# Two smaller last chunks, and Q placed by DMA, in a fused attention and MLP kernel

## The chip, the cores and the metric

The kernel runs on one core of one Trainium2 chip. The metric is the device time of the whole launch in microseconds (us). Lower is better. The kernel before took 1586.94 us, the median of three runs (1586.9, 1586.94 and 1588.01).

## The reference

The input is x, 2048 rows of 512 numbers in bf16. The same two blocks are applied twice, with the same weights both times, so there are two layers of "attention, then MLP":

```python
x = x + attention(layernorm(x))   # 32 heads of 16 numbers each
x = x + mlp(layernorm(x))         # 512 -> 1792, relu, -> 512
x = x + attention(layernorm(x))
x = x + mlp(layernorm(x))
```

```python
q, k, v = split(x @ wqkv)                      # wqkv: 512 x 1536
scores = einsum("hqd,hkd->hqk", q, k) * 16 ** -0.5
o = einsum("hqk,hkd->hqd", softmax(scores), v)
attention = o @ wo                             # wo: 512 x 512
mlp = maximum(h @ w1, 0) @ w2                  # w1: 512 x 1792, w2: 1792 x 512
```

All heads attend to all 2048 keys, so 2 x 32 x 2048 x 2048 scores have to be put through an exponential. That is 268 million of them, or 4096 blocks of 128 keys by 512 queries.

## The kernel before

**Engines.** TensorE (PE) does the products, ScalarE (ACT) does most of the exponentials, VectorE (DVE) does the rest of them with integer arithmetic on the bits (about one block in six), GpSimd (POOL) does small layer norm arithmetic and broadcasting DMAs, and the sync engine (SP) issues nearly all other DMAs. Each engine works through its own list in the order in which it is written. An instruction whose input is late holds up everything behind it on its engine.

**Chunks.** Queries are handled in chunks of 512 rows (`QS`). In the second layer (l = 1) the last 1024 rows are cut into four chunks of 256, numbered (1, 2) to (1, 5); `LAST` is 5. A chunk is gone through in four *runs*, one for each T in 0 to 3: a run holds the 128 columns of Q of eight heads. Each run has two *segments*, e = 0 and e = 1: the heads stand in pairs inside 32 partitions, and a segment works on one head of each pair. The buffer `qbuf[n % 2]` therefore holds Q twice, once with the odd heads masked to zero and once with the even ones. `q_masked` (line 676) writes both halves from the PSUM bank `ps_f` in one DVE operation of twice the width.

**The attention loop.** Each turn (a *slot*) of the loop from line 1267 takes three units of 128 keys by 512 scores in one group of 32 partitions. PE writes their scores (line 1396) to one of two PSUM tiles of three banks. ACT then takes the exponential of all three banks (a tile of 1536 columns), or of two (1024 columns) while DVE takes the third (line 1090 and the four steps from line 1131 on, for two blocks at a time: a *pair*). PE multiplies the results by V (line 983) into the bank `ps_o`. Where a chunk has 256 rows, a unit is two blocks of keys by 256 queries.

**The planner.** The order of all this is written out by the Python program itself, which keeps a model clock for PE, DVE and ACT. Products that are not attention (K, V, Q, the output projection, both MLP products) are cut into pieces that are put between the scores of the slots. `q_group` (682) is urgent as soon as the run before it begins. `h_group` (722) makes the first MLP product with weight tiles that SP loads in turn into four buffers (`load_w1`, 710). At the end of a segment `finish_segment` (867) copies `ps_o` to a buffer u, sends the row of sums through SP to a small tile, takes reciprocals there, sends them back, broadcasts them (POOL DMA at 927, or a shuffle on DVE at 937), and multiplies (913).

**The start.** The lines from 182 on load x and the weights. `load_w` (179) loads the K and Q columns of wqkv in one DMA of 512 KB each. Then come layer norm of the first 512 rows, transposes on PE, and the first K, Q and V products. On SP the order is: x, K's weights, x, `wo`, the 1792 KB of `w2` (195), four tiles of `w1` (714), and then the DMA transposes (571) of the normalised tiles `xnbuf[0..3]` of rows 512 on, which the DVE writes at line 528.

**The end.** After the last segment the code from line 1437 on finishes the last chunk of 256 rows without the planner: normalisation of the last segment, output projection, layer norm, and both MLP products, interleaved by tile of the hidden layer (lines 1501 to 1522), with all of `w1` kept in SBUF by then (`w1_last`).

Of the kernel before, what the change touches and what calls it, by code (L numbers as in the profile page):

```python
# [25 lines left out]
def kernel(  # L26
# [11 lines left out]
    P = 128  # L38
# [43 lines left out]
    X_ISSUE, X_LAG = 1400.0, 7500.0  # L82
    RSTD_LAG = 4000.0
    AHEAD = (8.0, 8.0)
    LATE = 0.0
# [22 lines left out]
    qmask = masks[:, 2:4]  # L108
    wqkv = sb([P, NDC, 3 * D], BF16, "wqkv")
    wo = sb([P, NDC, D], BF16, "wo")  # L110
# [67 lines left out]

    def load_w(engine, a):
        engine.dma_start(out=wqkv[:, :, a : a + D], in_=wq_src[:, :, a : a + D])  # L180

# [6 lines left out]
    nc.scalar.activation(out=warm[:], in_=warm[:], func=ACTF.Exp)  # L188
    load_w(nc.sync, D)
    load_w(nc.scalar, 0)  # L190
    load_x(nc.sync, (4, 5, 6, 7))
    load_w(nc.scalar, 2 * D)
    load_x(nc.sync, range(8, NTT))
    nc.sync.dma_start(out=wo[:], in_=A_wo[:, :].rearrange("(c p) f -> p c f", p=P))
    nc.sync.dma_start(out=w2[:], in_=B_w2[:, :].rearrange("(c p) f -> p c f", p=P))

    make_identity(nc, ident[:])
    for kb in range(NKB):
        nc.gpsimd.memset(vaug[0][kb][:, :, DH : DH + 2], 1.0)
    for kb in range(NKB - TPC):  # L200
        nc.gpsimd.memset(vaug[1][kb][:, :, DH : DH + 2], 1.0)


    wide = [True]
# [256 lines left out]
    HALF = TPC // 2  # L461
    for n in range(4):
        chunks[1, 2 + n] = (2 * TPC + n * HALF, HALF)
    LAST = 5

# [46 lines left out]
    def ln_root(tag, rows):  # L512
# [11 lines left out]
        stt(out=y, in0=t1, scalar=1.5, in1=y, op0=ALU.add, op1=ALU.mult)  # L524

    def ln_apply(tag, tt, i):
        n = ln_n(tag)
        nc.vector.tensor_scalar(
            out=xnbuf[i][:], in0=x_t[tt][:],
            scalar1=mv[n][:, i, 0:1], scalar2=ya_[n][:, i : i + 1],  # L530
            op0=ALU.subtract, op1=ALU.mult,
        )

    def ln_transpose(tag, i, b=None, at_bank=None):
        pt = bank().bitcast(BF16) if b is None else b
        for c in range(NDC):
            ins = nc.tensor.transpose(
                pt[:, c * P : (c + 1) * P], xnbuf[i][:, c * P : (c + 1) * P], ident[:]
            )
            if wide[0]:  # L540
                uses(ins, in_bank[0] if b is None else at_bank)
        mark(("xT", tag, i), "pe")
        return pt[:, 0 : NDC * P].rearrange("p (c f) -> p c f", c=NDC)
# [4 lines left out]
    def ln_rows(tag, tt, n, i):  # L548
# [10 lines left out]
        if i == n - 1:  # L559
# [6 lines left out]
            def apply(k):  # L566
                ln_apply(tag, tt + k, k)
                if not by_dma(tag):
                    return
                _, l, j = tag  # L570
                nc.sync.dma_start_transpose(
                    out=xnT[j][:, :, k * P : (k + 1) * P], in_=xnbuf[k][:]
# [13 lines left out]
    def ln_groups(tag, dst, at_column, n, war):  # L586
        groups = []
        for i in range(0, n, 2):
            hold = {}

            def piece(k):
                if not k % 2:
                    hold["b"] = bank()
                half = hold["b"].bitcast(BF16)[:, k % 2 * D : (k % 2 + 1) * D]
                ln_transpose(tag, k, half)
                if not k % 2:
                    return
                pt = hold["b"].bitcast(BF16).rearrange("p (i c f) -> p c i f", i=2, c=NDC)

                def fin():  # L600
                    a = at_column + (k - 1) * P
                    nc.vector.tensor_copy(
                        out=dst[:, :, a : a + 2 * P].rearrange("p c (i f) -> p c i f", i=2), in_=pt
                    )
                    for of in (k - 1, k):
                        mark(("xnT", tag, of))

                put_evac(609, fin)

            groups.append(  # L610
                group(
                    [(1.3, lambda k=k, piece=piece: piece(k)) for k in (i, i + 1)],
                    [("xT", tag, k) for k in (i, i + 1)] + [("xnT", tag, k) for k in (i, i + 1)],
                    [("xn", tag, k) for k in (i, i + 1)] + war,
                )
# [6 lines left out]
    def k_mms(T, j):  # L622
        return [(wqkv[:, c, D + T * P : D + (T + 1) * P], xnT[j][:, c, :]) for c in range(NDC)]

# [10 lines left out]
    def v_mms(kb):  # L635
        j, i = divmod(kb, TPC)
        return [
            (xnT[j][:, c, i * P : (i + 1) * P], wqkv[:, c, 2 * D : 3 * D]) for c in range(NDC)
        ]
# [29 lines left out]
    def q_mms(l, j, T):  # L669
        xj, a, w = columns(l, j)  # L670
        return [
            (wqkv[:, c, T * P : (T + 1) * P], xnT[xj][:, c, a : a + w]) for c in range(NDC)
        ]
# [8 lines left out]
    def q_group(n, l, j, T):  # L682
        xj, _, w = columns(l, j)
        cost = 90 + 2.09 * w

        def fin(b):
            q_masked(n, b, w)
            mark(("q", n))

# [20 lines left out]
    def load_w1(n):  # L710

        if n < len(chunks) * NF - NF + NW1:
            ft = n % NF
# [6 lines left out]
    w1_to_load = deque()  # L720

    def h_group(l, j, ft, war):
        n = (l * NQS + j) * NF + ft
        xj, a, w = columns(l, j)

        number = QS // w
        fts = range(ft, ft + number)
# [14 lines left out]
        def after():  # L742
            for f in range(number):
                load_w1(n + f + NW1)
            if w1_to_load:
                home, of = w1_to_load.popleft()
                nc.sync.dma_start(
                    out=home,
# [4 lines left out]
            [  # L753
                (w1buf[(n + f) % NW1][:, c, :], xnT[xj][:, c, a : a + w])
                for f in range(number) for c in range(NDC)
            ],
            fin, made_here,
            each(w // P, "xnT", ("ln2", l, j)) + war + [("w1", n + f) for f in range(number)],
            after=after, wide_by=w, sums=number,
        )  # L760
# [20 lines left out]
    def before(l, j):  # L781
# [3 lines left out]
        if not j:  # L785
            return 0, NQS - 1
        rows = chunks[l, j][0] % TPC
        return max(
            (l, b) for b in range(j)
            if chunks[l, b][1] == TPC or chunks[l, b][0] % TPC == rows  # L790
        )
# [3 lines left out]
    def rest_of_chunk(l, j):  # L795

        if (l, j) == (1, LAST - 2):
            for ft in range(NF):
                home = (
                    w1buf[((l * NQS + LAST) * NF + ft) % NW1] if ft < NW1  # L800
                    else (kt01 + kt2)[(ft - NW1) // 2][:, ft % 2, :].rearrange(
# [12 lines left out]
        )  # L814
        gs = [h_group(l, j, ft, war_h) for ft in range(0, NF, QS // w)]
        gs += [z_group(l, j, i) for i in range((l, j) == (1, LAST - 1), n)]
# [47 lines left out]

    sums_wait = [0]

    def finish_segment(sg, last):
# [16 lines left out]
        if n >= NU:  # L884
            run_until(("m", n - NU))
        u, r, c = ubuf[n % NU], rbuf[n % NU], cbuf[n % NU]
        lane = DH if e == 0 else DH - 1
# [32 lines left out]
        ended[l, j] = ended.get((l, j), 0) + 1  # L920
        quick = ended[l, j] == NT or sg["load"] is not None and sg["busy"]

# [39 lines left out]
        elif sg is segs[-2]:  # L962
            task(3100, direct_all, ots + [("m", n)], war + [("u", n)])
        else:
# [203 lines left out]
    for e in range(2):  # L1168
# [3 lines left out]
            op=ALU.add, axis=mybir.AxisListType.XY,  # L1172
        )
        nc.vector.tensor_scalar(
            out=qmask[:, e : e + 1], in0=mask[e], scalar1=SCALE * LOG2E * UNIT, scalar2=None,
            op0=ALU.mult,
# [382 lines left out]
```

The softmax here doesn't subtract the row's maximum and nothing guards it: scores larger than these inputs give would overflow.

## Time and profile before

The times come from one execution under the hardware profiler. Its span, from the first to the last instruction, is 1586.6 us; that execution took 1588.44 us as a whole, so 1.84 us lie outside the span.

| part of the span | us | ACT busy, us |
|---|---|---|
| start to the first exponential | 0 to 14.4 | 3.15 |
| first run of attention | 14.4 to 28.7 | 13.68 |
| attention, chunks of 512 for the most part | 28.7 to 1100 | 1066.34 |
| attention, chunks of 256 for the most part | 1100 to 1557.6 | 456.64 |
| after the last exponential | 1557.6 to 1586.6 | 5.55 |

| engine | busy, us | share of the span |
|---|---|---|
| ACT | 1545.3 | 97% |
| DVE | 1506.7 | 95% |
| PE | 1430.4 | 90% |
| POOL | 101.3 | 6% |

A busy PE is not PE at its peak[...]. "Idle before" in a row of the profile is time in which the engine stood still just before these instructions, and the name behind the arrow is what it waited for. The granted TensorE clock was 0.995 of full speed.

### The profile page before, as it was taken

To read this page: it belongs to the slowest core of one execution; us is meant where nothing else is said; L and a number is where in the kernel's file an instruction comes from. 1 tells how busy PE (TensorE), PEld (TensorE's weight loads), DVE (VectorE), ACT (ScalarE), POOL (GpSimd) and SP (SyncE) were. 2 spreads that over 40 slices of the span, in tenths; PEclk is the share of its full clock that TensorE was granted. 3 is DMA by queue.
4 is the path that set the end of the run, shared out by engine and by line. 5 is a ranking of instruction groups with operands and counts; after the bars stand their busy time and mean duration, and the time that the engine had idled before them with its cause. 6 is when DMAs were issued, how large, how long until landed. Compare 5 with 4: busy or idle time off the path is not lost.

```text
span 1586.6 us, 45174 instructions
## 1 busy us (share of the span) xinstructions
PE 1430.4 (90%) x19752; PEld 536.9 (34%) x19752; DVE 1506.7 (95%) x2910; ACT 1545.3 (97%) x1383; POOL 101.3 (6%) x240
## 2 busy tenths in 40 slices
PE   8888889998899989999899998888999999999898
PEld 3222223222233322322223222223334444544454
DVE  7899999999999999999899998899999999999994
ACT  7999999999999999999999999999999999999994
POOL 2000001001010010100100001001001000010100
PEclk9999999999999999999999999999999999999998
DMA  6001101111012120120101000000210111313030
GB/s 193 15 2 26 18 9 22 39 25 25 6 19 45 23 29 7 25 48 13 26 2 28 21 2 1 2 4 9 54 25 16 40 33 27 74 26 80 13 62 15
DMA packets 128885, 45.57 MB, mean 29 GB/s; under 512 B 117840, under 2 KB 125776, under 8 KB 128688
## 3 DMA queue, kind: packets, MB, share of 16 engines
q1 hardware_dynamic: 114752, 29.36, 8.6%
q0 software_dynamic: 12592, 12.02, 4.3%
q8 instruction: 154, 2.52, 0.7%
q10 hardware_dynamic: 1344, 1.31, 0.2%
q14 instruction: 43, 0.35, 0.1%
HBM read 24.38 MB, written 2.10 MB: 17 GB/s over the span
## 4 chain that ended last, share of the span: by engine, by line
ACT 81%; PE 8%; DVE 7%; issue 2%; DMA 1%; ACTq 0%; DVEq 0%
ACT e L1405 81%; PE ps_s L1396 3%; PE ps_f L446 2%; DVE lin L1090 2%; PE ps_o L983 2%; DVE step L1131 1%; PE ps_s L1458 1%; DVE cube L1146 1%; DVE cube L1142 1%; DMA wqkv<-in_A_wqkv_dram 1%; DMA r<-u 0%; DVE ht L736 0%; DVE q L676 0%; DVE ot L913 0%; DVE stats L481 0%
## 5 line engine op out<-in xcount | busy, mean ns | idle before, releaser
L1405 ACT ACTIVATE e<-ps_s 128x1536 bf16<-128x1536 f32 (+1 forms) x1366 | 1536.7, 1362 | 8.5 <-PE ps_s L1396 8.1
L1396 PE MATMUL ps_s<-q,ktp 32*128 32x512 bf16 (+1 forms) x6136 | 608.1, 341 | 112.4 <-ACT e L1405 99.2
L983 PE MATMUL ps_o<-e,vaug 128*32 128x512 bf16 (+1 forms) x4236 | 500.8, 346 | 14.1 <-DVE u L897 8.3
L1090 DVE TENSOR_SCALAR lin<-ps_s 128x512 int16<-128x512 f32 x702 | 478.3, 685 | 24.5 <-PE ps_s L1396 18.1
L1396 PEld LDWEIGHTS <-ktp 32*128 32x128 bf16 x6136 | 200.3, 92 | 563.6 <-issue 418.9
L1131 DVE TENSOR_SCALAR step<-lin 128x1024 int16<-128x1024 int16 x702 | 275.3, 419 | 1.9 <-PE ps_o L983 0.9
L983 PEld LDWEIGHTS <-vaug 128*32 128x32 bf16 x6052 | 173.8, 95 | 300.9 <-issue 282.2
L1142 DVE TENSOR_TENSOR cube<-step 128x1024 f16<-128x1024 bf16 x351 | 238.4, 683 | 1.6 <-PE ps_o L983 0.2
L1146 DVE TENSOR_TENSOR cube<-cube,lin 128x1024 bf16<-128x1024 f16 x351 | 238.0, 679 | 0.0
L446 PE MATMUL ps_f<-w,ht 128*32 128x512 bf16 x1624 | 151.6, 381 | 1.8 <-DVE x L768 0.5
L446 PE MATMUL ps_f<-xnT,w 128*32 128x512 bf16 (+1 forms) x2016 | 146.3, 345 | 5.8 <-DVE ht L736 3.6
L983 PE MATMUL ps_o<-step,vaug 128*32 128x512 bf16 (+1 forms) x884 | 151.0, 340 | 0.0
L983 PE MATMUL ps_o<-cube,vthird 128*32 128x512 bf16 (+1 forms) x836 | 148.9, 339 | 0.0
L983 PE MATMUL ps_o<-lin,vaug 128*32 128x512 bf16 (+1 forms) x884 | 125.9, 339 | 4.6 <-DVE u L897 3.2
L927 POOL DMA_DIRECT2D r<-u x59 | 43.1, 731 | 1168.6 <-DVE lin L1090 341.7
L446 PE MATMUL ps_f<-xnT,wqkv 128*32 128x512 bf16 (+1 forms) x1312 | 109.4, 365 | 6.2 <-DVE ktp L626 1.1
L446 PE MATMUL ps_f<-wo,ot 128*32 128x512 bf16 x960 | 90.3, 381 | 1.2 <-DVE x L700 1.2
L736 DVE TENSOR_SCALAR ht<-ps_f 128x512 bf16<-128x512 f32 x105 | 72.0, 685 | 2.3 <-PE ps_f L446 1.5
L446 PEld LDWEIGHTS <-w 128*32 128x32 bf16 x2016 | 57.5, 96 | 33.9 <-issue 18.7
L676 DVE TENSOR_TENSOR q<-ps_f,masks 128x1024 bf16<-128x1024 f32 (+1 forms) x51 | 53.6, 1052 | 9.1 <-PE ps_f L446 8.1
L446 PEld LDWEIGHTS <-ht 128*32 128x32 bf16 x1624 | 46.9, 96 | 25.3 <-issue 11.9
L983 PEld LDWEIGHTS <-vthird 128*32 128x32 bf16 x836 | 43.6, 95 | 33.5 <-issue 28.7
(103 smaller groups left out, 609.4 us busy)
## 6 DMA issues: line engine op xcount, KB each, us to landing
w<-in_B_w_dram SPq DMA_DIRECT2D x130, 128.0 KB
r<-u POOLq DMA_DIRECT2D x32, 256.0 KB, 7.3
r<-u POOLq DMA_DIRECT2D x27, 128.0 KB, 4.9
out_dram<-x SPq DMA_DIRECT2D x16, 128.0 KB
x<-in_A_x_dram SPq DMA_DIRECT2D x14, 128.0 KB
w<-in_B_w_dram SPq DMA_DIRECT2D x1, 1792.0 KB
ktp<-in_B_w_dram SPq DMA_DIRECT2D x10, 128.0 KB
wqkv<-in_A_wqkv_dram ACTq DMA_DIRECT2D x2, 512.0 KB
```

What stands on the lines that cost most here:

```text
L446: nc.tensor.matmul(out[cols], lhsT[:, cols], rhs, start=i % k == 0, stop=i % k == k - 1, tile_position=(0, 32 * g), skip_group_check=True,)
L676: return nc.vector.tensor_mul(out=qbuf[n % 2][:, :, 0:w], in0=b.rearrange("p (e q) -> p e q", e=1).to_broadcast((P, 2, w)), in1=qmask.rear ...
L736: nc.vector.tensor_scalar(out=out, in0=sums, scalar1=0.0, scalar2=None, op0=ALU.max)
L927: nc.gpsimd.dma_start(out=r[:, 0:width], in_=bass.AP(tensor=sums.tensor, offset=sums.offset, ap=[list(sums.ap[0]), [0, 32], [1, width]],),)
L983: nc.tensor.matmul(ps_o[32 * g : 32 * g + 32, 0 : sg["w"]], values[:, 4 * sg["T"] + g, 2 * e : 2 * e + 32], rhs, start=g not in sg["begun" ...
L1090: first = nc.vector.tensor_scalar(out=lin[which][:, half * QS : (half + 1) * QS], in0=src, scalar1=EXP_BIAS, scalar2=0.0, op0=ALU.add, op1 ...
L1131: nc.vector.tensor_scalar(out=stair, in0=line, scalar1=keep, scalar2=put, op0=ALU.bitwise_and, op1=ALU.bitwise_or,)
L1142: (609, lambda: nc.vector.tensor_mul(out=power, in0=mantissa, in1=mantissa)),
L1146: (609, lambda: nc.vector.tensor_mul(out=power.bitcast(BF16), in0=power, in1=line.bitcast(BF16))),
L1396: nc.tensor.matmul(b[:, a : a + sg["w"]], kt[32 * g : 32 * g + 32, kc : kc + P], qbuf[sg["n"] % 2][32 * g : 32 * g + 32, sg["e"], 0 : sg[" ...
L1405: ex = nc.scalar.activation(out=eb[:, 0 : place[m]], in_=b[:, 0 : place[m]], func=ACTF.Exp, scale=1.0 / (LOG2E * UNIT),)
L1458: uses(nc.tensor.matmul(out, lhsT, rhs, start=first, stop=last), b, needs=needs)
```

## The change

Four things are changed together.

- **Chunks.** The last 256 rows become two chunks of 128, (1, 5) and (1, 6), and `LAST` becomes 6. Units of these chunks are four blocks of keys by 128 queries. The tiles of `w1` that are kept for the end now serve chunk (1, 5) as well. The code after the last segment handles one tile of 128 rows, and it still finishes the MLP of the chunk before it.
- **Q.** The columns of the K and Q weights are interleaved at the start, so that the two heads of a pair stand on even and odd partitions. DVE then scales Q once into a spare tile (`xnbuf[3]`), and two DMAs on SP copy the even and the odd partitions to the two halves of `qbuf`, whose other partitions stay zero. Where `xnbuf[3]` is in use, the old operation is kept.
- **The start.** The weights for T = 0 are staged by SP and ACT and interleaved by two ACT copies; those for T = 1 to 3 are staged by six POOL DMAs and interleaved by six POOL copies. The staging space lies in `w2`, so the load of `w2` comes after all of the copies; it is still ahead of the `w1` tiles on SP.
- **Buffers of the normalisation.** u and r come from one ring of six, and where stored sums are added up, they stay where they are.

```diff
+    stage = w2[:].rearrange("p a f -> p (a f)")[:, 0 : 2 * 4 * NDC * P].rearrange(
+        "p (k t c f) -> p k t c f", k=2, t=4, c=NDC
+    )
+    def load_w(engine, k, T):
+        a = (1 - k) * D + T * P
+        engine.dma_start(out=stage[:, k, T], in_=wq_src[:, :, a : a + P])
+    def interleave(copy, k, T):
+        copy(
+            out=wkq[:, k, T].rearrange("p c (g d e) -> p (c g) e d", g=4, e=2),
+            in_=stage[:, k, T].rearrange("p c (g e d) -> p (c g) e d", g=4, e=2),
+        )
...
-    load_w(nc.sync, D)
-    load_w(nc.scalar, 0)
+    load_w(nc.sync, 0, 0)
+    load_w(nc.scalar, 1, 0)
     load_x(nc.sync, (4, 5, 6, 7))
-    load_w(nc.scalar, 2 * D)
+    nc.scalar.dma_start(out=wv[:], in_=wq_src[:, :, 2 * D : 3 * D])
+    for k in range(2):
+        interleave(nc.scalar.copy, k, 0)
     load_x(nc.sync, range(8, NTT))
     nc.sync.dma_start(out=wo[:], in_=A_wo[:, :].rearrange("(c p) f -> p c f", p=P))
-    nc.sync.dma_start(out=w2[:], in_=B_w2[:, :].rearrange("(c p) f -> p c f", p=P))
     make_identity(nc, ident[:])
+    nc.gpsimd.memset(qbuf[1][:], 0.0)
+    for T in range(1, 4):
+        for k in range(2):
+            load_w(nc.gpsimd, k, T)
...
+    for T in range(1, 4):
+        for k in range(2):
+            interleave(nc.gpsimd.tensor_copy, k, T)
+    nc.sync.dma_start(out=w2[:], in_=B_w2[:, :].rearrange("(c p) f -> p c f", p=P))
...
-    for n in range(4):
+    for n in range(3):
         chunks[1, 2 + n] = (2 * TPC + n * HALF, HALF)
-    LAST = 5
+    chunks[1, 5] = (3 * TPC + HALF, 1)
+    chunks[1, 6] = (3 * TPC + HALF + 1, 1)
+    LAST = 6
...
         def fin(b):
-            q_masked(n, b, w)
-            mark(("q", n))
+            if xn_waits[0]:
+                q_masked(n, b, w)
+                now_dve[0] += 13 + 1.045 * w
+                mark(("q", n))
+                return
+            qraw = xnbuf[TPC - 1]
+            nc.vector.tensor_scalar(
+                out=qraw[:, 0:w], in0=b, scalar1=SCALE * LOG2E * UNIT, scalar2=None, op0=ALU.mult
+            )
+            for e in range(2):
+                nc.sync.dma_start(out=qbuf[n % 2][e:P:2, e, 0:w], in_=qraw[e:P:2, 0:w])
+            mark(("q", n), lag=Q_LAG)
...
+    def per_group(w):
+        return min(QS // w, 2)
...
         if n >= NU:
-            run_until(("m", n - NU))
-        u, r, c = ubuf[n % NU], rbuf[n % NU], cbuf[n % NU]
+            run_until(("r", n - NU))
+        c = cbuf[n % NU]
+        def room():
+            buf, of = ring.popleft()
+            if of is not None:
+                run_until(("m", of))
+            ring.append((buf, n))
+            return buf
+        u = room() if sg["load"] is None else sg["load"]
+        r = room()
...
-        quick = ended[l, j] == NT or sg["load"] is not None and sg["busy"]
+        quick = ended[l, j] == NT or sg["load"] is not None and sg["busy"] or width == P
```

`xn_waits` counts the times that `xnbuf[3]` is written and not yet handed on. `quick` chooses the shuffle on DVE instead of the broadcasting DMA of POOL.

## The prediction

> **What bounds the kernel now.** I read the chain that ended last first, then the groups by shape, then the timelines of ACT, DVE and SP at both ends.
>
> The page: engine totals, the chain, and the exponential's row.
>
> ```profile
> PE 1430.4 (90%) x19752; PEld 536.9 (34%) x19752; DVE 1506.7 (95%) x2910; ACT 1545.3 (97%) x1383; POOL 101.3 (6%) x240
> ...
> ACT 81%; PE 8%; DVE 7%; issue 2%; DMA 1%; ACTq 0%; DVEq 0%
> ...
> L1405 ACT ACTIVATE e<-ps_s 128x1536 bf16<-128x1536 f32 (+1 forms) x1366 | 1536.7, 1362 | 8.5 <-PE ps_s L1396 8.1
> ```
>
> Between the first and the last exponential ACT stands still for only 8.5 us in all. So there are three ways to change the time: fewer ACT microseconds, a shift of the first exponentials, or a shorter tail. DVE (95%) matters only through the number of blocks that it takes over, or where it makes ACT wait.
>
> The groups kept apart by shape (count, busy us, mean ns):
>
> ```profile
> L1405 ACT ACTIVATE e<-ps_s 128x1536 bf16<-128x1536 f32 x663 | 1005.1, 1578 | 4.8 <-PE ps_s L1396 4.4 <-PE ps_o L983 0.3
> L1405 ACT ACTIVATE e<-ps_s 128x1024 bf16<-128x1024 f32 x702 | 760.8, 1159 | 3.6 <-PE ps_s L1396 3.6
> L676 DVE TENSOR_TENSOR q<-ps_f,masks 128x1024 bf16<-128x1024 f32 x35 | 42.7, 1220 | 8.8 <-PE ps_f L446 8.1 <-PE ps_s L1396 0.3
> ```
>
> One block moved from ACT to DVE saves ACT 1578 - 1159 = 419 ns.
>
> The timelines (start, duration) of SP, DVE and ACT at the start:
>
> ```profile
> 14.28 0.51 SPq L195 DMA_DIRECT2D w<-in_B_w_dram  x1
> 14.84 8.47 SPq L714 DMA_DIRECT2D w<-in_B_w_dram  x4
> 23.42 14.60 SPq L571 DMA_TRANSPOSE xnT<-xn  x8
> ...
> 22.46 1.37 DVE L528 TENSOR_SCALAR xn<-x,mv,ya 128x512 bf16<-128x512 bf16 x4
> 23.75 0.68 DVE L481 BATCH_NORM_STATS2 stats<-x 128x6 f32<-128x512 bf16 x1
> 24.35 0.69 DVE L662 CAST vaug<-ps_f 128x512 bf16<-128x512 f32 x1
> ...
> 27.18 0.68 DVE L626 CAST ktp<-ps_f 128x512 bf16<-128x512 f32 x1
> ...
> 28.67 12.20 ACT L1405 ACTIVATE e<-ps_s 128x1536 bf16<-128x1536 f32 x9 [0.26 <-PE ps_o L983]
> ```
>
> SP is held until 23.4 us by the `w2` and `w1` loads, and the exponential at 28.67 already follows the DVE's K cast at 27.18 closely: any DVE delay here reaches ACT.
>
> The tail, from the ACT and DVE timelines:
>
> ```profile
> 1555.54 2.10 ACT L1405 ACTIVATE e<-ps_s 128x1536 bf16<-128x1536 f32 x2 [0.16 <-PE ps_s L1396]
> ...
> 1580.64 0.42 DVE L1512 TENSOR_SCALAR ht<-ps_s 128x256 bf16<-128x256 f32 x1 [1.31 <-PE ps_s L1458]
> 1582.59 0.69 DVE L1525 CAST x<-ps_s 128x512 bf16<-128x512 f32 x1 [1.53 <-PE ps_s L1458]
> ```
>
> The last exponential ends at 1557.64, the span at 1586.6: a tail of 29 us. Its relus wait for PE (1.31 us each time), so PE sets the pace there.
>
> **What the Trainium skill says.** (1) "TensorE: Matmul & The Clock Gate", Back-to-back issue gap: a warm matmul takes N / 2.4 + 2.5 ns alone (56 at N = 128), about 81 ns at N = 128 in a stream with weight loads. The trace has 0.87 us for four matmuls of 256 columns and two of 512 in the tail; the formula gives 870 ns. (2) The same page, Architectural detail: ACT and DVE queues are strict FIFO. The DVE timeline agrees. (3) "DMA: Bandwidth & Descriptors", Queues, rings and completion order: descriptors are consumed in ring order. The landings agree: `w2` at 24.8 us, the `w1` tiles at 25.2 to 26.3, the first transpose, issued at 23.42, only at 27.0.
>
> **The change, part by part.** The order of the instructions on each engine is fixed when the program is built, so counts are exact.
>
> *Exponentials.* ACT gets 659 tiles of 1536 and 706 of 1024 columns, against 663 and 702: 4 x 0.419 = **-1.7 us**. DVE pays for the two more pairs (3.6 us each) with Q: 34 scalings at 0.69 instead of 1.22 us and 12 at 0.42 instead of 0.68 save 21 us. The 128-row chunks give some 8 us back (more copies, shuffles, products). DVE ends some 6 us lighter; that is off the path, hence no further gain.
>
> *Tail.* With one tile instead of two: one reciprocal and product less (1.3 us), but PE bounds that stretch: nine output matmuls at 0.216 behind two leftover hidden groups of chunk (1, 5) (64 matmuls, about 0.9 us, plus 0.3 for a relu on the same bank), so the copy of x starts 3.4 us after the last product with V, against 4.7 now: -1.3. Layer norm: one statistic (0.6), one aggregate (0.15) and one start offset less: -1.0. The 15 matmuls for the chunk before (3.3 us) stay hidden under layer norm; if they weren't, at most 0.5 us would show. The second tile's transposes and DVE copy go: -0.7. MLP: 14 steps of four matmuls of 128 and one of 512 columns, 0.44 us on PE, but a relu round trip of about 0.60 (matmul latency 0.22, DVE 0.28, semaphores) spans two steps, so I take 0.49 against 0.87: 14 x 0.38 = -5.3. Last copy: one of 0.58 on ACT instead of a second of 0.69 on DVE behind it: -0.3. Together -8.6; I take **-7.6**, since a relu with fewer columns may not shrink with them.
>
> *Start.* T = 0: the two ACT copies (0.59 each) are over before ACT's transposed tiles at 8.91; the two more reductions on DVE (0.2 each) lie before the first x lands at 3.4. Nothing there. The exponential at 14.43 follows the masked Q at 12.72, which is unchanged. POOL: memset to about 2.3; six DMA issues at 0.68 (the duration of its `r` broadcasts), to 6.5; 28 memsets (1.8), to 8.3; six copies. The nearest row, the mask builder, has 128 columns in 0.29; the page "GPSIMD Engine Reference", section 3.1, has 769 ns for 512 elements at best. I take 0.9, so 5.4, and POOL is done at 14 to 16. Its layer norm began at 16.0, so it stays. `w2` is issued about 15 instead of 14.3. The four `w1` issues, and then the two Q DMAs of run 1, follow behind it on SP. They land behind the `w1` data, at **27 us** (24.5 if `wo` drains faster, 31 if the POOL loads are slow). The new wait: the DVE's fourth `xn` (ended 23.8 now) writes `xnbuf[3]`, from which those DMAs read, so DVE stands until 27. Behind it on DVE are two statistics (1.36), the V cast of the fourth key block, two statistics, one copy and the K cast of T = 1. PE waits for the V cast, and the K product waits for its bank. K is ready at 27.0 + 0.4 + 1.36 + 0.69 + 1.36 + 0.69 + 0.69 = 32.2 instead of 27.86: **+4.4 us** on ACT. ACT never has slack to win it back. The next DVE and SP steps shift along with it.
>
> *Q in flight.* A scaling, two issues and a landing take some 4 us, against runs of 12 us and more; hidden. If a run had no lead, each would cost 4 us. Five later layer norms write `xnbuf[3]` four to eight DVE operations after a Q scaling, that is 2 to 4.5 us later, and may wait up to 1.5 us each; DVE's 5% of idle time takes most: **+1.0** (0 to 5). SP issues 477 DMAs instead of 353 (108 for Q, 16 for eight more segments' sums); after 60 us it waits far more than it issues.
>
> *Width 128 in the attention loop.* The score and V products, 256 columns so far, go in rounds of 128: +2.5 ns a round, some 790 rounds: 2 us of PE over 82 slots, under ACT: **+0.5**. The bound below is zero, the bound above is a rival. The ring of u and r only loosens waits: 0.
>
> Sum: -1.7 - 7.6 + 4.4 + 1.0 + 0.5 = -3.4, or 1583.2 on the span of 1586.6. The profiled execution took 1588.44 (1.84 around its span), 1.5 above the median of 1586.94; from the median the sum gives about **1583.5 us**.
>
> **Rivals.**
>
> *The start stalls longer.* The `r` broadcasts of POOL land 7.3 us after issue for 256 KB and 4.9 for 128 KB, 2.4 for each 128 KB more. At that rate six loads are in by about 19.5, the copies by 20.5, and Q lands at 30.5: +8, so 1587.4. Against it: those broadcasts read few partitions, whereas SP's `w1` tiles from HBM land 0.38 us apart.
>
> *PE bounds the 128-wide stage* (slower). If a round takes 81 ns instead of 56, 790 rounds cost 20 us. PE is busy 50.9 of 57 us from 1500 to 1557, about 11% free, 10 us over that stage of some 93 us. That leaves +10: 1593.8. It decides from about 69 ns a round. For it: 40 matmuls and 40 weight loads a slot instead of 23 of each. Against it: eight transposes of 128 columns, with weight loads, take 0.72 us with the last one's latency of 0.22.
>
> *No stall.* If `wo` and `w2` drain earlier, Q lands by 24: +1 instead of +4.4, 1580.4. For it: K and Q weights arrive over three queues. Against it: `w2` waits for POOL.
>
> **How the numbers follow.** Forecast 0.55, longer stall 0.20, PE bound 0.15, no stall 0.10. No change is within 0.2%, 3.2 us. The forecast's own range is 1580.5 to 1587.5: 0.34 faster, 0.19 within, 0.02 slower. The long stall, with +1 to +5 from waits that I sized small: 0.10 within, 0.10 slower. PE bound: 0.15 slower. No stall: 0.09 faster, 0.01 within. Sums: faster 0.43, within 0.30, slower 0.27. The range for 8 in 10 is 1579.0 to 1595.0.
>
> **What would show it.** After: a DVE gap at about 24 to 27 us before the fourth `xn`, released by the Q DMA; ACT idle 4 us near 28 to 33; a tail near 21 us from the last exponential; relu steps of 0.49 us; ACT as full from 1460 to 1550 as now. It would be wrong if ACT's idle time before exponentials grew by more than 8 us, at the start or in the 128-wide stage, or if the relu steps stayed near 0.87.

## The result, and the profile after

The changed kernel takes 1639.48 us (median of 4 runs, 1637.12 to 1646.51) against 1587.47 us (4 runs, 1586.9 to 1593.5) for the kernel before, measured on the same chip. The ratio is 1.0326 (95% interval 1.0285 to 1.0367). It is 52 us slower, where the prediction had it 3.4 us faster, and it lies far outside the predicted range. The profiled execution has a span of 1636.2 us.

The page of the changed kernel: engine totals, the chain that ended last, and the row of the exponentials.

```profile
PE 1465.2 (90%) x21212; PEld 554.4 (34%) x21215; DVE 1501.2 (92%) x2984; ACT 1553.2 (95%) x1386; POOL 109.3 (7%) x256
...
ACT 61%; DVE 16%; PE 15%; DMA 5%; issue 2%; SPq 1%; DVEq 0%; ACTq 0%; POOLq 0%
...
L1475 ACT ACTIVATE e<-ps_s 128x1536 bf16<-128x1536 f32 (+1 forms) x1366 | 1543.5, 1338 | 58.3 <-PE ps_s L1466 52.0
```

ACT's share of the chain has fallen from 81 to 61%, and its idle time before exponentials has risen from 8.5 to 58.3 us. So this is not a matter of more work: ACT waits for scores. What the scores themselves wait for is in the view of waits (engine and line, what it waited for: us in total, times, longest):

```profile
ACT e L1475 <- PE ps_s L1466: 52.0, 59, 6.5
...
PE ps_s L1466 <- DMA q<-xn: 25.2, 14, 6.4
```

The kernel before has no wait of the second kind, since Q came from DVE there. To place the loss in time, I took the start of the k-th exponential in both traces (both have 1366) and subtracted. The two columns on the right are two of the experiments below, against the same trace of before.

| exponential k (start in before, us) | changed - before, us | `chunks_only` - before | `landed` - before |
|---|---|---|---|
| 0 (14.4) | +1.1 | +0.5 | +1.1 |
| 12 (31.3) | +5.4 | +0.6 | +5.4 |
| 48 (75.2) | +8.0 | +0.6 | +6.3 |
| 375 (441.5) | +4.9 | +1.8 | +3.7 |
| 425 (497.2) | +10.0 | +1.8 | +4.9 |
| 875 (1002.0) | +11.2 | +1.7 | +1.7 |
| 925 (1061.0) | +21.9 | +1.7 | +5.2 |
| 975 (1117.2) | +21.8 | +1.7 | +4.2 |
| 1025 (1173.8) | +34.9 | +2.9 | +6.6 |
| 1275 (1455.5) | +33.4 | +0.6 | +6.0 |
| 1365 (1557.0) | +57.6 | +6.2 | +15.9 |
| end of the span | +49.6 | -2.8 | +7.0 |

In the changed kernel the loss comes in a few places: 4.3 us at the start, 2.2 before exponential 48, 5.1 between 375 and 425, 10.7 and 13.1 in two short stretches of the second layer, and 24.2 in the 128-wide stage. Between them the distance hardly moves. The tail gives 8.0 back. PE's 14 waits for Q lie in four of these places: one of 1.7 us before exponential 48, four with 3.9 in all in the first short stretch, two with 9.2 in the second, seven with 10.4 in the 128-wide stage. All fourteen Qs belong to a run that follows a short one: of 32 units, some 11 slots, because it goes over only four blocks of keys or is 128 wide. No Q behind a longer run makes PE wait.

Who is it that needs Q so early? Here is the longest wait, in the timelines of PE, ACT and DVE of the changed kernel (start, duration, instruction, and in brackets the idle time before it):

```profile
1191.01 0.39 PE L1466 MATMUL ps_s<-q,ktp 32*128 32x512 bf16 x2
1197.82 0.58 PE L1466 MATMUL ps_s<-q,ktp 32*128 32x256 bf16 x2 [6.42 <-DMA q<-xn]
...
1198.44 1.02 ACT L1475 ACTIVATE e<-ps_s 128x1024 bf16<-128x1024 f32 x1 [6.53 <-PE ps_s L1466]
...
1198.44 0.69 DVE L1155 TENSOR_SCALAR lin<-ps_s 128x512 int16<-128x512 f32 x1 [6.50 <-PE ps_s L1466]
```

Two of the slot's three units are 512 queries wide, so they belong to chunk (1, 1). The third is made of two blocks of 256 queries: it belongs to the next chunk, and DVE takes it (`lin`), while ACT's tile has two blocks. The run has not changed over here. The planner gave DVE one block of the *next* run ahead of time. The scaling of that Q ended at 1190.41 and its second DMA was issued at 1191.04. The condition by which the planner chooses (lines 1378 to 1382 of the changed kernel) is

```python
if (
    sg["l"] == mine["l"] and ahead.count(sg) + (sg is mine) > 1
    and at([("q", sg["n"])], "pe") is not None
    and ends < now_pe[0] + till * QS * 0.84 - 1300.0
):
```

It asks whether Q is planned at all. It doesn't ask when it lands: `Q_LAG` goes into the time that `at` returns, and that time is not compared with anything. The kernel before does the same, and its trace shows it. DVE and PE in the kernel before:

```profile
1022.15 1.22 DVE L676 TENSOR_TENSOR q<-ps_f,masks 128x1024 bf16<-128x1024 f32 x1
...
1024.28 0.69 DVE L1090 TENSOR_SCALAR lin<-ps_s 128x512 int16<-128x512 f32 x1 [0.75 <-PE ps_s L1396]
...
1023.41 0.82 PE L1396 MATMUL ps_s<-q,ktp 32*128 32x512 bf16 x9 [0.62 <-ACT e L1405]
```

The nine products at 1023.41 are one slot's three scores, made three times over, as the planner does where PE has time to spare. One of each three reads the Q that DVE finished at 1023.37. With Q made on DVE the block can be had at once. I went through all 52 masked Qs of before in this way, score by score in program order: eleven, one of them the very first, have their first use less than 4 us after they are done, and six of them within 0.4 us, four of these in a row (1010 to 1048 us). The others have leads of 4 to 43 us.

**Theory A**, then: DVE's blocks of the next run are taken while its Q is in flight, PE waits for the DMA with everything behind it, and ACT runs dry. **Theory B**: Q is simply late at the change of runs, because its DMAs stand behind other DMAs on SP. **Theory C**: much of the loss is not Q at all, but PE in the 128-wide stage. Later a **theory D** was added, on the part of the loss that goes beyond the waits.

### The profile page after: what moved, and what is told of

Read it like the earlier page. It is cut to its first block, busy times and chain, and to the rows that moved or that the text cites. A ratio compares the mean times of both kernels' runs of the same rounds, so it can differ in the third digit from the quotient of the medians.

```text
span 1636.2 us, 48456 instructions
## 1 busy us (share of the span) xinstructions
PE 1465.2 (90%) x21212; PEld 554.4 (34%) x21215; DVE 1501.2 (92%) x2984; ACT 1553.2 (95%) x1386; POOL 109.3 (7%) x256
## 4 chain that ended last, share of the span: by engine, by line
ACT 61%; DVE 16%; PE 15%; DMA 5%; issue 2%; SPq 1%; DVEq 0%; ACTq 0%; POOLq 0%
ACT e L1475 61%; PE ps_s L1466 6%; PE ps_o L1048 5%; DVE lin L1155 4%; PE ps_f L470 4%; DMA q<-xn 3%; DVE step L1196 2%; DVE cube L1207 2%; DVE cube L1211 2%; DMA x<-in_A_x_dram 1%; DVE ht L783 1%; DVE xn L727 1%; PE ps_s L1528 1%; DMA r<-u 1%; DVE u L962 0%
## 5 line engine op out<-in xcount | busy, mean ns | idle before, releaser
L1475 ACT ACTIVATE e<-ps_s 128x1536 bf16<-128x1536 f32 (+1 forms) x1366 | 1543.5, 1338 | 58.3 <-PE ps_s L1466 52.0
L1466 PE MATMUL ps_s<-q,ktp 32*128 32x512 bf16 (+2 forms) x6579 | 621.7, 333 | 120.9 <-ACT e L1475 86.4
L1048 PE MATMUL ps_o<-e,vaug 128*32 128x512 bf16 (+2 forms) x4670 | 511.3, 335 | 9.6 <-DVE u L962 5.6
L1048 PE MATMUL ps_o<-step,vaug 128*32 128x512 bf16 (+2 forms) x962 | 161.2, 333 | 1.2 <-DVE step L1196 1.2
L470 PE MATMUL ps_f<-xnT,w 128*32 128x512 bf16 (+2 forms) x2080 | 155.4, 348 | 6.3 <-DVE ht L783 4.4
L1048 PE MATMUL ps_o<-cube,vthird 128*32 128x512 bf16 (+2 forms) x886 | 149.6, 332 | 2.5 <-DVE cube L1211 2.5
L1048 PE MATMUL ps_o<-lin,vaug 128*32 128x512 bf16 (+2 forms) x962 | 132.1, 332 | 7.3 <-DVE u L962 4.9
L470 PE MATMUL ps_f<-xnT,wkq 128*32 128x512 bf16 (+2 forms) x1376 | 110.7, 360 | 7.5 <-DVE vaug L696 2.7
L992 POOL DMA_DIRECT2D r<-u x46 | 34.6, 752 | 943.9 <-DVE lin L1155 255.3
L783 DVE TENSOR_SCALAR ht<-ps_f 128x512 bf16<-128x512 f32 (+1 forms) x110 | 74.2, 674 | 7.6 <-PE ps_f L470 7.2
L470 PEld LDWEIGHTS <-wkq 128*32 128x32 bf16 x1376 | 38.7, 97 | 35.3 <-issue 22.8
```

Of the source, the lines that this page charges most:

```text
L470: nc.tensor.matmul(out[cols], lhsT[:, cols], rhs, start=i % k == 0, stop=i % k == k - 1, tile_position=(0, 32 * g), skip_group_check=True,)
L783: nc.vector.tensor_scalar(out=out, in0=sums, scalar1=0.0, scalar2=None, op0=ALU.max)
L992: nc.gpsimd.dma_start(out=r[:, 0:width], in_=bass.AP(tensor=sums.tensor, offset=sums.offset, ap=[list(sums.ap[0]), [0, 32], [1, width]],),)
L1048: nc.tensor.matmul(ps_o[32 * g : 32 * g + 32, 0 : sg["w"]], values[:, 4 * sg["T"] + g, 2 * e : 2 * e + 32], rhs, start=g not in sg["begun" ...
L1466: nc.tensor.matmul(b[:, a : a + sg["w"]], kt[32 * g : 32 * g + 32, kc : kc + P], qbuf[sg["n"] % 2][32 * g : 32 * g + 32, sg["e"], 0 : sg[" ...
L1475: ex = nc.scalar.activation(out=eb[:, 0 : place[m]], in_=b[:, 0 : place[m]], func=ACTF.Exp, scale=1.0 / (LOG2E * UNIT),)
```

## The experiments

The kernel before was measured again beside each group of experiments: its median was 1589.43 us for experiments 1 to 4, 1589.36 for 5 to 8, 1588.31 for `busy_wait` and `few_rows`, and 1590.42 for `full_array_wait`. Ratios are to that value.

**1. `landed`: only the choice of DVE's blocks is changed.**

```diff
-                            and at([("q", sg["n"])], "pe") is not None
+                            and (at([("q", sg["n"])], "pe") or 1e18) <= now_pe[0]
```

> The changed kernel, in which the planner hands DVE a block of a run only when its own clock says that this run's Q has landed (so far: as soon as the Q product is planned). By count ACT then has 685 tiles of 1536 and 680 of 1024 columns instead of 659 and 706: +26 x 0.419 = +10.9 us. Theory A (DVE's blocks are taken from the next run while its Q is still in flight, PE's scores wait for the DMA, and ACT with them): PE's waits for Q fall from 25 us to under 5, ACT's idle time before exponentials from 58 to about 20, and the time is 1639 - 44 + 11 = about 1606. Theory B (Q is late at the run change itself, because its DMAs stand behind others on SP): nothing of that changes, 1640 to 1650. Theory C (PE bounds the 128-wide stage): only the losses before 1220 us go, about 1639 - 24 + 11 = 1626.

Measured: 1594.72 us, ratio 1.0036 (1.0025 to 1.0047). One line takes back 45 of the 52 us. The exponentials' row on the page of this run:

```profile
L1475 ACT ACTIVATE e<-ps_s 128x1536 bf16<-128x1536 f32 (+1 forms) x1366 | 1546.7, 1366 | 13.3 <-PE ps_s L1466 8.2
```

And the only line of its waits that still names the Q DMAs:

```profile
DVE xn L557 <- DMA q<-xn: 5.4, 4, 3.1
```

PE has no wait for Q left. All 108 Q DMAs are still there, on SP, in the same places behind the same transfers, so B falls. The time is 11 us better than expected, because the loss that went with the waits was larger than the 44 us I had put in.

**2. `masked`: every Q by the masked product.** Interleaved weights, chunks and start stay.

```diff
-            if xn_waits[0]:
+            if True:
                 q_masked(n, b, w)
```

> The changed kernel with its chunks, interleaved weights and start, but every Q by the masked product on DVE, with no Q DMA. ACT has 671 tiles of 1536 and 694 of 1024 columns (+12 x 0.419 = +5 us on the changed kernel). Theory A, and B: all waits for Q go, 1639 - 52 + 5 - (start, if its +8 comes from the Q DMAs) = 1584 to 1592. Theory C: the 24 us of the 128-wide stage stay, about 1608 to 1616. For the start: 8 us late still means POOL's interleaving or the weights, 0 to 2 us late means the DVE's wait for the Q DMAs.

Measured: 1585.12 us, ratio 0.9973 (0.9964 to 0.9983). No exponential up to the 1000th is more than 1 us late, the start included. So POOL's interleaving costs at most 1 us, and the start's 4.3 us need the Q DMAs.

**3. `chunks_only`: the kernel before with the chunks, the ring and the kept copy, and nothing of Q.** (The diff is that of the change without its hunks on `wkq`, `load_w`, `interleave`, `qmask` and `q_group`.)

> The kernel before with the chunks of 128 (and the ring of u and r, and the kept copy) alone: Q masked on DVE, weights loaded as before. ACT has 671 and 694 tiles against 663 and 702 (+3.4 us). Theory A and B: the tail's -8 us, no loss elsewhere, 1587.5 - 8 + 3.4 + 0.5 = about 1583. Theory C: the 128-wide stage loses some 14 to 24 us by itself, 1597 to 1607.

Measured: 1584.97 us, ratio 0.9974 (0.9964 to 0.9984). C falls: the 128-wide stage (from exponential 1282 to the last) takes 99.3 us against 94.3, of which eight more tiles of 1536 columns explain 3.4 (8 x 0.426, from the tiles' start-to-start medians of 1.330 and 0.904 us). About 1.6 us are left, which the narrower products would explain; that was not tested by itself. This kernel and `masked` are the two that beat the kernel before, by 0.3%. Part of that goes with a higher granted clock, whose cause these runs don't show: its median is 0.997 in both, against 0.994 in the kernel before beside them.

**4. `q_only`: the kernel before with Q by DMA and interleaved weights, chunks of 256.**

> The kernel before with Q by DMA and interleaved weights alone, chunks of 256 as before. ACT has 653 and 712 tiles (-4.2 us). Theory A and B: the start's +8 and the +24 at 1013 to 1083 and 1166 to 1208 us appear, and no gain in the tail: 1587.5 + 8 + 24 - 4 = about 1615. Theory C, in which the 128-wide stage makes nearly half of the loss: the same 1615. If Q costs nothing here and needs the narrow runs to hurt: about 1591.

Measured: 1633.75 us (1625.57 to 1639.73), ratio 1.0285 (1.0253 to 1.0316). Q alone costs 44 us, without any 128-wide chunk. The sum in the expectation was 19 us too small. The trace (span 1623.5, the low end of the runs) has eight waits of PE for Q with 18.1 us, at the same two stretches of the second layer and at the start.

**5. `pool_queue`: Q's DMAs on another queue.**

```diff
-                nc.sync.dma_start(out=qbuf[n % 2][e:P:2, e, 0:w], in_=qraw[e:P:2, 0:w])
+                nc.gpsimd.dma_start(out=qbuf[n % 2][e:P:2, e, 0:w], in_=qraw[e:P:2, 0:w])
```

> The changed kernel with the Q DMAs issued from POOL's queue instead of SP's; the order of blocks and of all other work is the changed kernel's own (659 and 706 tiles). Theory A: the Q is taken before it can land whatever the queue, so PE's waits for Q stay near 25 us or grow with POOL's issue, and the time is 1630 to 1660. Theory B (Q stands behind other DMAs on SP): the waits fall to under 8 us and the time to about 1600.

Measured: 1644.71 us (two executions), ratio 1.0341 (1.0316 to 1.0367). PE's waits for Q are 25.7 us in 14 places, against 25.2 in 14. So the waits don't hang on SP's other traffic.

**6. `landed_less`: a block may be taken earlier by 4 us of the planner's clock.**

```diff
-                            and (at([("q", sg["n"])], "pe") or 1e18) <= now_pe[0]
+                            and (at([("q", sg["n"])], "pe") or 1e18) <= now_pe[0] + 4000.0
```

> As landed, but a block may be taken 4 us of planner's time before the moment at which the planner holds Q for landed, that is about 2 us after the scaling; 667 and 698 tiles. Theory A: a scaling, an issue and the landing took 3.5 to 4 us in the waits of the changed kernel (7 in one), so some of its waits come back with 1 to 2 us each, 5 to 12 us in all, and with them the halved clock of PE behind them: 1600 to 1618, between the two. If the waits are what costs and not the number of blocks, the fewer tiles (-18 x 0.419 = -7.5 us against landed) don't show.

Measured: 1590.99 us, ratio 1.0001 (0.9988 to 1.0014). The waits did not come back: there is none of PE for Q. So 2 us after the scaling by the planner's clock are enough in this order of blocks. The gain of some 6 us on `landed` fits the fewer wide tiles (667 against 685, 7.5 us by their prices), but the order of blocks changed too. My expectation missed in both.

**7. `landed_first_masked`: as `landed`, with the Q of run 1 masked.**

```diff
-            if xn_waits[0]:
+            if xn_waits[0] or n == 1:
```

> As landed, and the Q of run 1 by the masked product, so that DVE's fourth xn has no DMA to wait for at the start; 683 and 682 tiles (-0.8 us). If the 4.5 us by which the exponentials 7 to 12 came late are this wait, as the prediction had it: 1594.7 - 4.5 - 0.8 = about 1589.4, and no exponential before the 40th is over 1.5 us late. If the weights or POOL set the start: 1594.

Measured: 1599.97 us (1595.11 to 1602.81), ratio 1.0057 (1.0034 to 1.0079): slower than `landed`, not faster. The stall at the start is gone: exponentials 12 and 48 are 1.0 and 1.2 us late instead of 5.4 and 6.3 (at most 1.9 in between, so the expected 1.5 was a little too low). But the planner arranges everything after it anew, and the granted clock is lower: 0.989 to 0.992 in the four executions, against a median of 0.994 in `landed`. In the trace (span 1593.3, below the median) about 4 us are lost near 650 us, where DVE's fourth `xn` waits 2.03 us for a Q DMA, PE then waits 2.12 us for the transposed tile, and the clock is 0.50 for the next 6 us. So this run shows the cause of the start's delay, but not a gain.

**8. `long_runs`: Q by DMA only behind runs of at least 20 slots, masked elsewhere, with the condition of `landed`.**

> As landed, but Q goes by DMA only where the run before it has at least 20 slots, and by the masked product elsewhere (the starts of both layers and the 128-wide stage); 663 and 702 tiles, 8 fewer wide ones than masked and chunks_only. Theory A: no waits for Q, no stall at the start, and ACT's tiles decide: 1585.0 - 8 x 0.419 = about 1581.6. If a Q DMA has another cost (SP, the later layer norms), 1585 or more.

Measured: 1591.05 us, ratio 1.0009 (0.9999 to 1.0019). PE has no wait for Q, but there is no gain over masking either; the expectation was 9 us too low. Up to the 128-wide stage, the distance to the trace of before grows mainly in two places: by 3.6 us between exponentials 100 and 150, and by 2.2 between 925 and 950. In both the granted clock is 0.50, for 13.7 us from 160 us on and for 10.2 us from 1064 us on, with no PE wait for Q. What brings it down there, these runs don't show. The longest single wait, at 402 us, where DVE waits 3.95 us for a broadcast of r and PE 3.56 us for DVE, adds under 0.5 us to the distance, since the kernel before waits there too.

**9 and 10. The part beyond the waits.** The waits sum up to 25.2 us. The losses at the same places sum up to 50 (2.2, 10.7, 13.1 and 24.2), of which some 4 in the 128-wide stage are six more wide tiles and the narrower products (experiment 3). The windows of the changed kernel around its first wait in the second layer show more (PE busy, weight loads, DVE, ACT, POOL, then the granted clock, the DMA share and GB/s):

```profile
1021.50:1022.30 0.80, 0.04 (x3) 0.00 (x1) 0.00 (x0) 0.80 (x1) 0.00 (x0) 0.80 0.27 91
1022.30:1024.00 1.70, 1.70 (x10) 0.34 (x12) 0.66 (x1) 0.80 (x2) 0.00 (x0) 0.50 0.10 34
1024.00:1026.00 2.00, 2.00 (x15) 0.24 (x9) 0.62 (x2) 1.50 (x2) 0.00 (x0) 0.50 0.00 0
1026.00:1028.00 2.00, 2.00 (x17) 0.37 (x17) 1.65 (x4) 1.42 (x3) 0.00 (x0) 0.50 0.04 4
```

PE stood still for 0.76 us, and then ran at half clock for some 6 us; a round of scores took 0.61 us instead of 0.39, and ACT, which had to wait 0.90 us for the first tile, waited 0.50, 0.52 and 0.28 us for the next ones. Not every wait is like this one: at eight of the 14 the clock fell to 0.50 during the wait or within 2.4 us after it; at the other six, of 0.44 to 1.71 us, it stayed at 1.0. In all, up to the last exponential, the trace of the changed kernel has 85 us at half clock in 13 stretches, and that of before 14 us in three. Theory D: this halved clock makes the rest of the loss. To test it, PE was kept busy during the wait:

```diff
...
             turn = sorted(zip(place, now), key=in_turn)
+            coming = {
+                x[1][0]["n"] for x in turn if made[("q", x[1][0]["n"])][1] > now_pe[0]
+            } - warmed
+            if coming and turn[0][1][0]["n"] not in coming:
+                warmed.update(coming)
+                late = max(made[("q", n)][1] for n in coming) - 2500.0 - now_pe[0]
+                turn[:0] = turn[:1] * max(int(late / MM), 0)
...
```

> The changed kernel with its own order and its own waits for Q, but ahead of the first block of a Q that is still in flight PE repeats another block's score product of the same slot, 9 to 16 times (163 products at 0.216 us, 35 us in all, at 14 places), so that most of each wait is filled with work. The result of the repeated product is the same. Theory D (the loss beyond the waits themselves comes from PE's clock, which the windows show halved for some 5 us after each wait): the clock stays at 1.0, each of the 14 places costs the wait alone, and the time falls from 1639 to about 1610 to 1620. Rival (refilling the two score tiles makes the rest of the loss): 1639 or, as the repeats are longer than some waits, up to 1650.

Measured: 1642.68 us, ratio 1.0336 (1.0305 to 1.0367), no better. But the experiment had not done what it was for. PE still waited 11.4 us for Q, in five places, and the clock fell all the same. Two windows of `busy_wait`:

```profile
1024.00:1027.00 3.00, 3.00 (x18) 1.26 (x17) 0.00 (x0) 0.85 (x1) 0.00 (x0) 0.87 0.13 44
1027.00:1030.00 3.00, 3.00 (x18) 0.46 (x19) 0.69 (x1) 1.50 (x2) 0.00 (x0) 0.50 0.00 0
```

PE is busy all the time here, and the clock still falls to 0.50. The repeated product contracts over 32 rows in one row group, a quarter of the array. So the next kernel repeats a product over the whole array instead, for as many columns:

```diff
...
+                    nc.tensor.matmul(
+                        b[:, a : a + wide_by], ident[:], wo[:, 0, 0:wide_by], start=True, stop=True
+                    )
```

> As busy_wait, but what PE repeats at the 14 places is a product over the whole array (128 rows of contraction, 128 columns of weights, 9 to 16 times 512 columns or as many columns in narrower ones), written where the late score goes and then overwritten by it; in busy_wait it was a product of 32 rows, a quarter of the array, and the windows showed the clock at half there although PE was never idle. Theory D' (the clock follows the use of the array; the halved clock after each wait makes the loss beyond the waits): the clock stays at or near 1.0 at these places, and the time falls from 1639 to 1605 to 1622. Rival (refilling the score tiles makes the rest): 1635 to 1650 with the clock at 1.0.

Measured: 1629.28 us, ratio 1.0253 (1.0226 to 1.0281). The window of its first such place in this stretch:

```profile
1018.00:1021.00 3.00, 3.00 (x18) 1.09 (x16) 0.00 (x0) 0.65 (x1) 0.00 (x0) 1.00 0.08 28
1021.00:1024.00 3.00, 2.75 (x35) 0.81 (x35) 2.34 (x4) 2.87 (x3) 0.00 (x0) 1.00 0.00 0
```

The clock stays at 1.0, and the mean over the span is 0.994 instead of 0.974. ACT, after its one wait, is full again. PE still waited 3.8 us for Q, in two places. The gain over the changed kernel is 0.7% of the ratio, 11 to 12 us, although the fill (163 x 0.216 = 35 us) is longer than the waits were (25). By the two intervals that gain is uncertain by some 8 us. Against `busy_wait`, which has the same number of repeats in the same places, it is 0.8%. In the stretch from exponential 875 to 925 the four places now cost 9.6 us with 2.7 us of fill each, no more than PE's stops; in the changed kernel four waits of 0.76 to 1.50 us, 3.9 in all, cost 10.7. So a halved clock behind a wait is a real part of the loss, about 12 us of it by these medians, and more if the longer fill is allowed for. The time lies between the two forecasts: the expected 1605 to 1622 was too hopeful, and the rival's 1635 to 1650 too high. How the remainder divides between the waits and the refilling of the score tiles, these runs don't separate.

The executions of the kernel before support the same theory from another side. Of the 55 beside experiments 1 to 4, the seven with a granted clock of 0.997 or more took 1586.3 us on average, and the seven at 0.990 took 1593.8: about 1 us for each 0.001. By that rate the 0.974 of the changed kernel, against 0.995, is an estimated 20 us, about what the loss exceeds the waits by (46 - 25). It is a correlation, not an experiment.

**11. `few_rows`: latency or bytes?** Q is masked on DVE, and two DMAs of four rows each stand where Q's DMAs stood.

```diff
+            q_masked(n, b, w)
...
             for e in range(2):
-                nc.sync.dma_start(out=qbuf[n % 2][e:P:2, e, 0:w], in_=qraw[e:P:2, 0:w])
+                nc.sync.dma_start(
+                    out=qbuf[n % 2][1 - e : P : 32, e, 0:w], in_=qbuf[n % 2][3 - e : P : 32, e, 0:w]
+                )
```

> The changed kernel with the masked product for every Q, followed by two DMAs on SP of four rows each (zeros onto zeros of the same buffer, 4 KB instead of 64 KB), in the changed kernel's order of blocks; nothing reads the fourth xn buffer. If the latency of a DMA makes the wait: PE's waits for Q stay at 14 with 20 to 30 us in all, and the time is 1625 to 1645 (the start's 4.5 us are shorter). If the bytes of Q make it: under 8 us of waits, about 1600.

Measured: 1617.31 us (two executions), ratio 1.0183 (1.0156 to 1.0209). PE and its weight loads wait 21.5 us for these DMAs in 17 places (11.5 in 11 and 10.0 in 6), the longest 2.6 us. A sixteenth of the bytes leaves most of the waits, so they are latency for the greater part; what goes is the longest, of 6.4 us. (The masked product takes 0.5 us longer than the scaling, which holds these DMAs up somewhat.) The changed kernel's own trace agrees: at its waits the score follows the end of the scaling by 1.8 to 3.5 us where a DMA moves 64 KB, and by 1.8 to 3.8 us where it moves 16 KB. The Trainium skill ("DMA: Bandwidth & Descriptors", Anatomy of one DMA) has, for DMAs issued by GpSimd, a fixed part of about 2 us and the bytes on top, which for 64 KB at its rate would be an estimated 0.15 us; the DMAs here are issued by SP and show the same pattern. The time lies below the expected 1625, partly because the start has no stall here.

## Why the prediction was wrong, step by step

**The step that failed: "Q in flight".** The prediction said: "A scaling, two issues and a landing take some 4 us, against runs of 12 us and more; hidden." The flight was sized well enough: at the waiting places, from the end of the scaling to the score that it released, it took 1.8 us in the shortest case, mostly 2 to 4, and 7.4 in the longest. What was wrong is the other side of the comparison. The lead of a Q is the time to its *first use*, and I took the length of the run for it. DVE's pairs use it while the run before still goes on. At the 14 places the first slot that is mostly the new run's own comes 6 to 19 us after the end of the scaling, so without the early blocks these flights would have been hidden, as predicted; the early block stood ahead of all that, and had to wait until Q landed, 1.8 to 7.4 us after the scaling. The prediction even had the right price, "If a run had no lead, each would cost 4 us", but counted no places and made no rival of it. Fourteen places at 4 us are 56 us; the loss at these places was some 46. That these come near each other is partly luck: the waits themselves were 25 us, and the rest followed behind them. The evidence lay in the trace of before, in the eleven Qs used within 4 us of the masked product. The changed order of instructions showed it as well: there a slot with two units of 512 columns and one of 256 waits for the DMA of the run that has not begun.

**"Five later layer norms write `xnbuf[3]` ... may wait up to 1.5 us each; DVE's 5% of idle time takes most: +1.0 (0 to 5)".** The mechanism was right, and the size wrong. Four such waits came, three of them under 1 us, and one of 3.30 us; between exponentials 375 and 425, where that one lies, ACT lost 5.1 us. DVE in the changed kernel:

```profile
467.23 0.41 DVE L557 TENSOR_SCALAR xn<-x,mv,ya 128x512 bf16<-128x512 bf16 x1 [3.30 <-DMA q<-xn]
```

PE waited 2.5 us behind it for DVE's `cube`, and its clock fell to 0.50 for 6.8 us. DVE's 5% of idle time, an average, did not absorb this one wait.

**The start, +4.4.** Right, in size and by its own steps: between exponentials 6 and 12 the distance grows by 4.5 us. The view named beforehand shows it (DVE in the changed kernel):

```profile
26.06 0.41 DVE L557 TENSOR_SCALAR xn<-x,mv,ya 128x512 bf16<-128x512 bf16 x1 [1.91 <-DMA q<-xn]
...
31.11 0.69 DVE L660 CAST ktp<-ps_f 128x512 bf16<-128x512 f32 x1 [0.56 <-PE ps_f L470]
```

Q landed at 26 us instead of 27, and the K cast ends at 31.8 instead of 32.2. `landed_first_masked` takes it away by masking that one Q. The first exponential is 1.1 us late besides, which the sum had at nothing.

**The tail, -7.6.** Right: from the start of the last exponential to the end of the span it is 21.6 us instead of 29.6, so -8.0, and -9.0 in `chunks_only`. The relus on DVE come every 1.00 us, two steps of the hidden layer apart, so a step takes 0.50 against the forecast 0.49:

```profile
1629.34 0.29 DVE L1582 TENSOR_SCALAR ht<-ps_s 128x128 bf16<-128x128 f32 x1 [0.71 <-PE ps_s L1528]
1630.33 0.29 DVE L1582 TENSOR_SCALAR ht<-ps_s 128x128 bf16<-128x128 f32 x1 [0.71 <-PE ps_s L1528]
```

**Exponentials, -1.7.** The counts were exact:

```profile
L1475 ACT ACTIVATE e<-ps_s 128x1536 bf16<-128x1536 f32 x659 | 991.3, 1556 | 22.8 <-PE ps_s L1466 18.0 <-PE ps_o L1048 3.7
L1475 ACT ACTIVATE e<-ps_s 128x1024 bf16<-128x1024 f32 x706 | 754.2, 1137 | 35.5 <-PE ps_s L1466 34.0 <-PE ps_o L1048 0.6
```

But the gain belongs to a plan in which DVE takes blocks too early. `landed` pays for not doing so with 685 wide tiles, 11 us by the tiles' prices. With Q masked there are 671, and with the shorter delay of `landed_less` 667. So the time that DVE saves on Q buys at most a few blocks: DVE is only 92% busy in `landed`, against 95% before.

**Width 128, +0.5.** At most about +1.6, by what `chunks_only` leaves over. The rival "PE bounds the 128-wide stage" is out. The rival "the start stalls longer" is out too (4.3, not 8), and so is "no stall".

**What the prediction named as a sign of being wrong** was the right one: "if ACT's idle time before exponentials grew by more than 8 us, at the start or in the 128-wide stage". It grew by 50. The rivals had no case with Q late in the middle of the kernel, which is where 24 of the 52 us went; the upper end of the range came from PE's pace alone. The sum of -3.4 is right as arithmetic, but the times of the three rivals stand 0.3 us too high against it: they start from 1583.8 and not from 1583.5. That is no part of the miss.

**The parts by themselves.** Chunks: 4.5 us gained (`chunks_only`). Q by DMA: 44 us lost (`q_only`). Their sum, 40, is 12 short of the 52: the narrow runs of the 128-wide stage are short again, and seven of the 14 waits lie there.

## What to carry to other kernels

Before an operation on an engine is replaced by one that lands later, measure in the old trace how soon each result is first used, for every use and not for the typical one; the length of a stage is only an upper bound. Where a planner decides the order, look for each test that asks whether something is "made", and see whether it reads the time. And price a wait of PE above its own length: here, with two score tiles of slack, 25 us of waiting went with some 46 us of loss, nearly two for each.

## What the runs showed of the hardware

- PE's clock can be halved after pauses much shorter than the stretch at half clock: a wait of 0.76 us was followed by some 6 us at 0.50. The Trainium skill ("TensorE: Matmul & The Clock Gate", What's actually happening) has the array throttled after an idle window of about 3.4 us. Here a much shorter pause inside a stream of narrow products was enough, so for this kernel the measurement decides. But such a pause need not do it: six of the 14 waits, of up to 1.71 us, left the clock at 1.0, and so did 18 of the 21 pauses of 0.7 us or more that PE makes between 30 and 1550 us in the kernel before. What tips it isn't shown.
- Being busy doesn't keep the clock up. A 4 us stream of 32-row products (a quarter of the array's rows) let it fall to 0.50, with no idle time; a 2.75 us stream of products over the whole array in the same place held it at 1.00. Over the whole span the granted clock was 0.973 in the first kernel and 0.994 in the second. That row use is the cause was tested by this one pair only.
- A strided DMA from SBUF to SBUF of 16 to 64 KB in rows of every other partition took 0.46 to 0.61 us to issue on SP in most cases, up to 2.4 in some. At the waits, its consumer was released 1.8 to 3.8 us after the source was ready, and once after 7.4. With 4 KB most of that stays.
